# Row maxima turned by VectorE instead of TensorE, and an output projection in half-height tiles, in an attention block with a gated MLP

## The chip, the core and the metric

The kernel runs on one core of a Trainium2 chip. A core has TensorE (PE: matmuls, whose weights are loaded by a separate instruction, PEld), VectorE (DVE), ScalarE (ACT), GpSimd (POOL) and SyncE (SP, which issues most DMAs). Each engine works through its own list of instructions in order; semaphores join them. Matmul results go to PSUM, which has eight banks of 128 x 512 fp32 values. The metric is the device time of one execution in microseconds, as the median of several runs.

## What is computed

One transformer block over 2048 tokens of width 512, all in fp32, with 32 heads of 16 and an MLP of width 1376:

```python
xn = _layernorm(x)
qkv = (xn @ wqkv).reshape(B, S, 3, H, Dh)          # S 2048, H 32, Dh 16
scores = einsum("bhqd,bhkd->bhqk", q, k) * Dh ** -0.5
p = softmax(scores)
s = einsum("bhqk,bhkd->bhqd", p, v).reshape(B, S, D) @ wo
g = silu(gelu(xn @ w1 + b1) @ w2 + b2)
out = x + s * g
```

## The kernel before

**Splitting.** An fp32 product is made from rounded operands: a high part h and the rest l, and three matmuls h·h, h·l, l·h (`mm3`, L76). For the scores the three terms lie on top of each other in the contraction: 16 rows each of qh, ql, qh against kh, kh, kl, that is 48 rows.

**Units.** Queries are cut in 4 chunks of 512, heads in 8 groups of 4. A pair (group, chunk) is a unit u, 32 in all. For each unit the scores are computed twice. The first time (`s_one`, `s_op`; "S") they come out with queries on partitions, and DVE takes row maxima from PSUM (L185). The second time (`t_one`, L722; "T") they come out with keys on partitions, with two more contraction rows in which the negated maximum of the query stands, as high and low part against ones; so 50 rows. ACT takes the exponential (L724), and the weighted sums `pv_step` (L787; "V") follow on TensorE, whose 17th column gives the denominators.

**Turning the maxima.** The maxima of a unit lie as 128 queries x (4 heads x 4 query tiles). `s_end0` (L235) reduces and negates them (L240, DVE) and has POOL split them into high and low part, `nmh`, 128 x 32 (L243, L244). They are needed as rows of 512 queries. `s_end1` (L257) turns them by a matmul against an identity into 32 x 128 in a PSUM bank; `s_end2` (L262) copies them to SBUF (`mh`; ACT in the early stage, DVE afterwards) and stores them to DRAM (`mh_d`, L268). `load_mh` (L147) loads them later into the two rows of the T operand. In the early stage the bank comes from the ring of the S tiles (`s_tile`), afterwards from the ring of the T tiles (`t_tile`, L707: `ps_m` and three of `ps_t` in turn).

**Row halves.** Operands of at most 64 rows use half of the array's rows. Such matmuls are issued for rows 0 to 63 and for rows 64 to 127 (a = 0 and a = 1 in the code). When one half adds to a bank that the other has written, the second must wait until the first is done; a tiny instruction on another engine that waits for the one and releases the other is put between (`mark`, L583, on ACT or DVE; in the middle stage a POOL `nop`, L217).

**Stages.** (1) Layer norm, its transposes and the first products. (2) An order made by a planner (L290 to L323): MLP and projections in row halves (L573), into which `fill` (L546) puts S matmuls at row counts that follow from `ROWS`; a turning takes a place in this order, and `put` shifts the counts by it. The first 576 S matmuls (LEAD = 144, four each), so the maxima of the first 9 units, are made here; eight of the units are turned here. (3) A loop over 512 steps n (L944). A step has four T of unit n // 16, a V of the step before, and, until step 491, three S in whole or in halves (`ORDER`, L40). Turnings come behind a V, through `flush` (L161). `at(n, f, ..., pos)` puts other work into step n, behind the T number pos (L897).

**The output projection.** In steps 492 to 511 (DONE = 492) ten of the 16 token tiles (NW = 10) are projected, each in two steps: `w_token` (L859) rounds the tile's attention output into `oh` and `ol` (ACT, POOL), `w_mul` (L870) has six full matmuls of 128 rows per step behind the fourth T (12 per tile, L79), and `w_out` (L891) multiplies by the gate (DVE, L883), adds x (POOL, L888) and stores (SP, L889). `gate` (L845) makes silu's factor from `gx`, which `load_gx` (L834) fills; `gx` is a ring of four buffers here. Results go to the ring of the S banks, three by then. Two more tiles and the last chunk of four follow after the loop, where the last unit's division ends last.

Of the kernel before, what the change touches and what calls it, by code (L numbers as in the profile page):

```python
# [8 lines left out]
F32 = mybir.dt.float32  # L9
F32R = mybir.dt.float32r  # L10
AF = mybir.ActivationFunctionType
# [21 lines left out]
LEAD = 144  # L33
NW = 10
EARLY = 4
DONE = 492
FILL0 = 38
# [4 lines left out]
KB = 3  # L42
# [5 lines left out]
def fused(ctx: ExitStack, tc: tile.TileContext, x, wqk, wv, wo, w1, b1, w2, b2, out):  # L48
    nc = tc.nc
# [15 lines left out]
    mh_d = dpool.tile([NG * NCH, 2, GH, CH], F32, name="mh_d")  # L65

    ident_r = keep.tile([P, P], F32R, name="ident_r")
# [13 lines left out]
            if then:  # L81
                then()

    QS, QT, MX, NM, MH = {}, {}, {}, {}, {}
# [68 lines left out]
    made = [0, 0]  # L153
    done = {u: 0 for u in range(NU)}
    later, ended, errands, sent = [], [], [], set()

    def tick():
        for e in later:
            e[0] -= 1

    def flush():  # L161
        while later and later[0][0] <= 0:
            u = later.pop(0)[1]
            run_off()
            s_end1(u)
            s_end2(u)

    def at_of(job):
        u, st, p = job
# [29 lines left out]
    def s_one(a):  # L199
        made[a] += 1  # L200
        s_whole(heads[made[a] - 1], a)
# [29 lines left out]
    def run_off():  # L231
        while put_off:
            put_off.pop(0)()
# [21 lines left out]
    prog = {}  # L255

    def s_end1(u):  # L257
        pm = s_tile()[0] if "seen" in prog else t_tile()
        nc.tensor.matmul(pm[:2 * GH * NCH, :P], NM.pop(u).rearrange("p i a -> p (i a)"), ident_r, start=True, stop=True)  # L259
        MH[u] = pm  # L260

    def s_end2(u):  # L262
        mh = qring.tile([2 * GH * NCH, P], F32, name="mh", bufs=1)
        if "seen" in prog:
            nc.scalar.activation(mh, MH.pop(u)[:2 * GH * NCH, :P], AF.Copy)
        else:
            nc.vector.tensor_copy(mh, MH.pop(u)[:2 * GH * NCH, :P])
        nc.sync.dma_start(mh_d[u].rearrange("i j (q s) -> (i j q) s", s=P), mh)  # L268
        sent.add(u)

    sa = ExitStack()
# [31 lines left out]
    for j in range(len(pairs)):  # L303
        for h in range(2):
# [4 lines left out]
            due = next((i for i in range(j, len(pairs)) if is_m[i]), len(pairs))  # L309
# [212 lines left out]
    qring = ctx.enter_context(tc.tile_pool(name="qring", bufs=2, side="right"))  # L522
# [16 lines left out]

    prog.update(n=0, pe=0, seen=0)  # L540
    writer = {}
    s_when, put, row = [], [0], [0, 0]
    ndown = sum(1 for e in plan if e[0] == "down")
    ROWS = 12 * (4 * VQ + 2 * len(pairs)) + 6 * ndown - 10 + 2 * LEAD - 2 * (LEAD // 16 - 1) - FILL0

    def fill(a):  # L546
        due = FILL0 + put[0] + sum(made) * ROWS // (4 * LEAD)
        if sum(made) < 4 * LEAD and row[a] >= due and (made[0] <= made[1]) == (a == 0):
            taken()
            if later and later[0][0] <= 0:  # L550
                put[0] += 2
                u = later.pop(0)[1]
                s_end1(u)
                s_end2(u)
# [205 lines left out]
    wb = ctx.enter_context(tc.tile_pool(name="work_b", bufs=2))  # L760
# [4 lines left out]
    wo_h = kp.tile([P, KT, D], F32R, name="wo_h")  # L765
    wo_l = kp.tile([P, KT, D], F32R, name="wo_l")

    WR = {}

    def load_wo(k):  # L770
        WR[k] = wb.tile([P, 2, D], F32, name="gx", bufs=4)[:, 0]
        nc.sync.dma_start(WR[k], wo[k * P:(k + 1) * P, :])

    def wo_high(k):
# [51 lines left out]
    GX, OTS, PW, homes = {}, {}, {}, {}  # L826

    def home(i):
        if i not in homes:
            homes[i] = (slot(i, (P, KT, D)) if i < KB else  # L830
                        keep_r.tile([P, 2 * KT, D], F32, name="kt0"))
        return homes[i]

    def load_gx(t):  # L834
        i = 2 * (t % NCH)
        if t < NW:
            GX[t] = wb.tile([P, 2, D], F32, name="gx", bufs=4)
        elif t < NT - NCH:
            GX[t] = home(KB)[:, i:i + 2]
# [8 lines left out]
        nc.vector.scalar_tensor_tensor(g, e, 1.0, g, op0=OP.add, op1=OP.mult)  # L848

    def w_round(blocks, src, lo):  # L850
        oh = wb.tile([P, KT, P], F32R, name="oh", bufs=3)
        ol = wb.tile([P, KT, P], F32R, name="ol", bufs=3)
# [17 lines left out]
    def w_mul(t, ks, parts=(0, 1)):  # L870
        if t not in PW:
            PW[t] = [ps_t.tile([P, CH], F32, name="pst") if NW <= t < NT - NCH or i else
                     ps_m.tile([P, CH], F32, name="ps") if t == NT - 1 else s_tile()[0]
                     for i, cs in enumerate(cols(t))]
        for i, cs in enumerate(cols(t)):
            if i in parts:
                for k in ks:
                    mm3(PW[t][i][:, :cs.stop - cs.start], OTS[t, k], (wo_h[:, k, cs], wo_l[:, k, cs]),
                        k == 0, k == KT - 1)

    def w_gate(t, i=0):
        gx, cs = GX[t], cols(t)[i]
# [14 lines left out]
    def at(n, f, *a, pos=3):  # L897
        todo.setdefault((n, pos), []).append((f, a))

    KS = tuple(range(KT))  # L900
# [21 lines left out]
            at(16 * u + (31 if u < NU - 2 else 22), o_div, u, nc.gpsimd)  # L922
    T3 = range(NT - NCH, NT)
    late = range(NW, NT)
    for t in range(NW):
        n = DONE + 2 * t
        at(n - 4, load_gx, t)
        at(n - 2, w_token, t)
        at(n, w_mul, t, KS[:2])
        at(n, gate, t)  # L930
        at(n + 1, w_mul, t, KS[2:])
        at(n + 1, w_out, t, nc.gpsimd)
    for i, t in enumerate(late):
        n = L - 2 * len(late) - 1 + 2 * i
        at(n - 4, load_gx, t)
# [8 lines left out]
    for n in range(L + 1):  # L944
        ua, ka = divmod(n, 16)
        want = due(n) - due(n - 1)
        i = 0
# [71 lines left out]
```

## Time and profile before

| | us |
|---|---|
| median of 3 runs | 1590.88 (1590.16 to 1591.05) |
| the profiled execution: its time | 1589.65 |
| its span, first to last instruction | 1587.9 |
| matmuls of line 259 (turning), count | 32, 0.25 each |
| copies of the turned maxima | 8 on ACT (L265), 24 on DVE (L267), 0.27 each |
| DVE reductions of line 185 | 2048, 0.685 each |

The page counts an engine as busy while an instruction of it is under way, and matmuls overlap in time, so PE is shown full nearly everywhere, and the granted TensorE clock is 0.999 of full speed. In the views below, an instruction row gives start and duration, engine, line and operation, the tiles written and read, shapes (`64*128 64x512` is 64 rows by 128 columns of weights and 512 moving columns) and a count; neighbouring rows of one kind are merged, and then the duration reaches from the first start to the last end. A group's row gives busy time, mean ns of one and, behind the bar, idle time of the engine ahead of it with what released it.

### The profile page before, as it was taken

How to read it: one execution, taken by the hardware profiler on the slowest of the kernel's cores; microseconds unless marked ns; L12 is line 12 of the kernel's file. 1: busy time of each engine (PE TensorE's matmuls, PEld its weight loads, DVE VectorE, ACT ScalarE, POOL GpSimd, SP SyncE). 2: the span in 40 equal slices, each digit the busy share in tenths (PEclk: the TensorE clock that was granted, in tenths of full speed). 3: DMA queues.
4: the chain of work that ended last, by engine and by line, in shares of the span. 5: the costliest groups of instructions: out<-in, count | busy, mean ns of one | idle time of the engine just before them, and what ended most of it. 6: DMA issues, size and time to landing. Idle time of an engine off the chain costs nothing.

```text
span 1587.9 us, 32482 instructions
## 1 busy us (share of the span) xinstructions
PE 1577.7 (99%) x12146; PEld 954.9 (60%) x12146; DVE 1382.6 (87%) x2267; ACT 1256.4 (79%) x2524; POOL 378.7 (24%) x398
## 2 busy tenths in 40 slices
PE   9999999999999999999999999999999999999998
PEld 7899989999995444444444444444444444444445
DVE  7489888888988999999999999999999999999734
ACT  4333433444339999999999999999999999999984
POOL 4145575755641001001100200100010000000144
PEclk9999999999999999999999999999999999999999
DMA  6625443354422113111511411221141111110262
GB/s 206 150 59 138 131 137 98 127 154 127 130 83 75 39 33 70 31 36 35 86 31 31 69 35 37 53 49 29 27 78 26 31 29 37 35 29 22 65 198 89
DMA packets 76798, 116.93 MB, mean 74 GB/s; under 512 B 25156, under 2 KB 26436, under 8 KB 75464
## 3 DMA queue, kind: packets, MB, share of 16 engines
q1 hardware_dynamic: 73180, 102.42, 23.4%
q0 software_dynamic: 3264, 12.35, 4.1%
q8 instruction: 96, 1.57, 0.4%
q14 instruction: 62, 0.51, 0.1%
q10 hardware_dynamic: 196, 0.07, 0.0%
HBM read 84.35 MB, written 25.97 MB: 69 GB/s over the span
## 4 chain that ended last, share of the span: by engine, by line
PE 98%; DVE 1%; DMA 0%; issue 0%; ACT 0%; SPq 0%; DVEq 0%; POOLq 0%; ACTq 0%
PE pv L787 32%; PE pst L722 22%; PE ps L573 13%; PE ps L179 9%; PE pst L573 7%; PE ps L722 7%; PE ps L79 4%; PE pv L573 2%; PE pst L79 1%; DVE slot L74 0%; DMA xt<-in_x 0%; DVE st L407 0%; PE pst L259 0%; PE ps L259 0%; DVE xn L421 0%
## 5 line engine op out<-in xcount | busy, mean ns | idle before, releaser
L185 DVE TENSOR_REDUCE mx<-ps 128x2 f32<-128x512 f32 x2048 | 1299.3, 685 | 137.3 <-PE ps L179 53.3
L724 ACT ACTIVATE slot<-pst 128x512 f32<-128x512 f32 x1533 | 833.3, 612 | 5.6 <-PE ps L179 1.1
L787 PE MATMUL pv<-slot,vsb 128*17 128x512 f32 (+1 forms) x4096 | 539.2, 598 | 0.0
L179 PE MATMUL ps<-kt,slot 48*128 48x512 f32 x1364 | 383.6, 370 | 0.1
L722 PE MATMUL pst<-qt,kt 50*128 50x512 f32 x1149 | 380.1, 431 | 0.5 <-DVE gt L655 0.3
L722 PEld LDWEIGHTS pst<-qt,kt 50*128 50x128 f32 x1149 | 191.5, 184 | 264.7 <-ACT slot L724 250.6
L724 ACT ACTIVATE slot<-ps 128x512 f32<-128x512 f32 x515 | 314.8, 612 | 10.3 <-PE pst L722 7.4
L179 PEld LDWEIGHTS ps<-kt,slot 48*128 48x128 f32 x1364 | 225.1, 184 | 2.1 <-POOLq L217 0.4
L573 PE MATMUL ps<-slot,w1h 64*128 64x512 f32 x1088 | 220.4, 393 | 0.0
L179 PE MATMUL ps<-kt,qz 48*128 48x512 f32 x512 | 214.7, 420 | 0.0
L179 PE MATMUL ps<-slot,slot 48*128 48x512 f32 x598 | 167.8, 368 | 0.0
L722 PE MATMUL ps<-qt,kt 50*128 50x512 f32 x387 | 164.1, 426 | 0.0
L573 PEld LDWEIGHTS ps<-slot,w1h 64*128 64x128 f32 x1088 | 153.0, 185 | 6.8 <-ACT junk L587 1.0
L573 PE MATMUL ps<-slot,w1l 64*128 64x512 f32 x544 | 143.0, 393 | 0.0
L367 POOL TENSOR_TENSOR hl<-hg,hh 128x512 fp32r<-128x512 f32 x76 | 96.9, 1298 | 131.5 <-ACT hh L366 92.6
L722 PE MATMUL pst<-qt,slot 50*128 50x512 f32 x384 | 120.1, 426 | 0.0
L787 PEld LDWEIGHTS pv<-slot,vsb 128*17 128x17 f32 (+1 forms) x4096 | 68.7, 96 | 82.8 <-issue 29.4
L587 ACT ACTIVATE junk<-ident_r 1x1 f32<-1x1 f32 x92 | 18.0, 196 | 126.1 <-PE pst L573 122.9
L722 PEld LDWEIGHTS ps<-qt,kt 50*128 50x128 f32 x387 | 71.1, 184 | 75.5 <-ACT slot L724 57.7
L722 PEld LDWEIGHTS pst<-qt,slot 50*128 50x128 f32 x384 | 65.9, 184 | 78.0 <-ACT slot L724 73.0
L179 PEld LDWEIGHTS ps<-kt,qz 48*128 48x128 f32 x512 | 93.7, 183 | 17.9 <-DVE mx L185 0.6
L179 PEld LDWEIGHTS ps<-slot,slot 48*128 48x128 f32 x598 | 98.7, 184 | 1.0
(150 smaller groups left out, 1659.4 us busy)
## 6 DMA issues: line engine op xcount, KB each, us to landing
raw<-in_w SPq DMA_DIRECT2D x88, 256.0 KB
qk_h<-hh SPq DMA_DIRECT2D x32, 256.0 KB
qk_l<-hl SPq DMA_DIRECT2D x32, 256.0 KB
qt<-qk_h SPq DMA_DIRECT2D x128, 64.0 KB
slot<-qk_h SPq DMA_DIRECT2D x92, 64.0 KB
xt<-in_x SPq DMA_DIRECT2D x16, 256.0 KB
g_d<-gt POOLq DMA_DIRECT2D x16, 256.0 KB, 3.0
qt<-qk_l SPq DMA_DIRECT2D x64, 64.0 KB
```

The costliest lines, as they stand in the source:

```text
L79: nc.tensor.matmul(ps, lhs[a], rhs[b], start=first and n == 0, stop=last and n == 2)
L179: return nc.tensor.matmul(ps[:, c0:c0 + w], QS[u][r, p, qi * P:(qi + 1) * P], kts[u // NCH % KB][p][r, k0:k0 + w], start=True, stop=True).ins
L185: nc.vector.tensor_reduce(MX[u][:, 2 * p:2 * p + 2, qi, ki][:, heads, parts], ps.rearrange("p (n c) -> p n c", c=HC), axis=AX.X, op=OP.max)
L367: nc.gpsimd.tensor_sub(hl, raw, hh.bitcast(F32))
L573: i = nc.tensor.matmul(ps, lhs[r], rhs[r], start=first, stop=last).ins
L587: i = nc.scalar.activation(junk[:, :1], ident_r[:1, :1].bitcast(F32), AF.Copy).ins
L722: nc.tensor.matmul(ps, kts[g % KB][p][r, k * P:(k + 1) * P], QT[u][r, p, :], start=True, stop=True)
L724: nc.scalar.activation(PT[u, k][:, 2 * p + a, :], ps, AF.Exp, scale=SCALE)
L787: nc.tensor.matmul(PV[u][32 * j:32 * j + w, :], vsb[:, k, h:h + w], PT[u, k][:, j, :], start=(k == 0), stop=(k == NT - 1))
```

## The change

Maxima are turned by one DVE instruction that transposes each 32 x 32 block of the 128 x 32 tile. Block b then holds, on partition 32 b + r, row r of the maxima for the 32 queries 32 b to 32 b + 31; the store puts the blocks together in DRAM, in 128 pieces of 128 B. The matmul, the PSUM bank and the copy go; `fill` no longer gives the turning a place.

The ten token tiles are projected two at a time over four steps, in 64-row tiles: tile t on rows 0 to 63 and tile t + 1 on rows 64 to 127 for two steps, then the other way round. Each of the 12 full matmuls of a tile becomes two of 64 rows, 240 in place of 120. They stand in groups of four behind the first, second and third T of a step. A POOL `nop` waits for the last matmul of the second step, and the first ones of the third step wait for it. Loads, rounding and output of the two tiles are moved with them: `w_token` of the second tile behind the first T of the step before, both `w_out` at the end of the fourth step. `oh` and `ol` get four buffers instead of three, the `gx` ring three instead of four, and every fourth tile's `gx` lies in a buffer of the keys that is free by then.

```diff
     def fill(a):
-        due = FILL0 + put[0] + sum(made) * ROWS // (4 * LEAD)
+        due = FILL0 + sum(made) * ROWS // (4 * LEAD)
...
             if later and later[0][0] <= 0:
-                put[0] += 2
-                u = later.pop(0)[1]
-                s_end1(u)
-                s_end2(u)
-                return
+                s_end1(later.pop(0)[1])
             s_one(a)
...
     def s_end1(u):
-        pm = s_tile()[0] if "seen" in prog else t_tile()
-        nc.tensor.matmul(pm[:2 * GH * NCH, :P], NM.pop(u).rearrange("p i a -> p (i a)"), ident_r, start=True, stop=True)
-        MH[u] = pm
-
-    def s_end2(u):
-        mh = qring.tile([2 * GH * NCH, P], F32, name="mh", bufs=1)
-        if "seen" in prog:
-            nc.scalar.activation(mh, MH.pop(u)[:2 * GH * NCH, :P], AF.Copy)
-        else:
-            nc.vector.tensor_copy(mh, MH.pop(u)[:2 * GH * NCH, :P])
-        nc.sync.dma_start(mh_d[u].rearrange("i j (q s) -> (i j q) s", s=P), mh)
+        mh = qring.tile([P, 2 * GH * NCH], F32, name="mh", bufs=1)
+        nc.vector.transpose(mh, NM.pop(u).rearrange("p i a -> p (i a)").bitcast(F32))
+        nc.sync.dma_start(mh_d[u].rearrange("i j (q b s) -> b (i j q) s", b=NCH, s=2 * GH * NCH), mh)
         sent.add(u)
...
+    def w_half(t, part, third):
+        two = (t, t + 1)
+        if part == 0 and third == 0:
+            for b in two:
+                PW[b] = [s_tile()[0]]
+        side, ks = divmod(part, 2)
+        ops = [(k, i, j) for k in KS[2 * ks:2 * ks + 2] for i, j in ((0, 0), (0, 1), (1, 0))]
+        for n in (2 * third, 2 * third + 1):
+            for a in range(2):
+                b, r, (k, i, j) = two[a ^ side], slice(64 * a, 64 * a + 64), ops[n]
+                op = nc.tensor.matmul(PW[b][0], OTS[b, k][i][r], (wo_h, wo_l)[j][r, k], start=part == 0 and n == 0,
+                                      stop=part == 3 and n == 5).ins
+                if part == 2 and n == 0:
+                    tc.add_manual_dep(op, turned[t].name, SYNC, reason="other row tile")
+        if part == 1 and third == 2:
+            turned[t] = nc.gpsimd.nop().ins
+            tc.add_manual_dep(turned[t], op.name, SYNC, reason="row tile done")
...
-    for t in range(NW):
+    for t in range(0, NW, 2):
         n = DONE + 2 * t
-        at(n - 4, load_gx, t)
-        at(n - 2, w_token, t)
-        at(n, w_mul, t, KS[:2])
-        at(n, gate, t)
-        at(n + 1, w_mul, t, KS[2:])
-        at(n + 1, w_out, t, nc.gpsimd)
+        for b in range(2):
+            at(n - 3 + b, load_gx, t + b)
+            at(n - 2 + b, w_token, t + b, pos=3 * (1 - b))
+            at(n + b, gate, t + b)
+        for part in range(4):
+            for third in range(3):
+                at(n + part, w_half, t, part, third, pos=third)
+        for b in range(2):
+            at(n + 3, w_out, t + b, nc.gpsimd)
```

More of the change, by code (lines that the diff above doesn't have):

```diff
@@ L82, in mm3 @@
                 then()
-    QS, QT, MX, NM, MH = {}, {}, {}, {}, {}
+    QS, QT, MX, NM = {}, {}, {}, {}
     SYNC = mybir.DependencyInfo(mybir.DependencyClass.Sync, mybir.DependencyReason.DATA)
@@ L541, in fused @@
     writer = {}
-    s_when, put, row = [], [0], [0, 0]
+    s_when, row = [], [0, 0]
     ndown = sum(1 for e in plan if e[0] == "down")
-    ROWS = 12 * (4 * VQ + 2 * len(pairs)) + 6 * ndown - 10 + 2 * LEAD - 2 * (LEAD // 16 - 1) - FILL0
+    ROWS = 12 * (4 * VQ + 2 * len(pairs)) + 6 * ndown - 10 + 2 * LEAD - FILL0
     def fill(a):
-        due = FILL0 + put[0] + sum(made) * ROWS // (4 * LEAD)
+        due = FILL0 + sum(made) * ROWS // (4 * LEAD)
         if sum(made) < 4 * LEAD and row[a] >= due and (made[0] <= made[1]) == (a == 0):
@@ L550, in fill @@
             if later and later[0][0] <= 0:
-                put[0] += 2
-                u = later.pop(0)[1]
-                s_end1(u)
-                s_end2(u)
-                return
+                s_end1(later.pop(0)[1])
             s_one(a)
@@ L770, in load_wo @@
     def load_wo(k):
-        WR[k] = wb.tile([P, 2, D], F32, name="gx", bufs=4)[:, 0]
+        WR[k] = wb.tile([P, 2, D], F32, name="gx", bufs=3)[:, 0]
         nc.sync.dma_start(WR[k], wo[k * P:(k + 1) * P, :])
@@ L835, in load_gx @@
         i = 2 * (t % NCH)
-        if t < NW:
-            GX[t] = wb.tile([P, 2, D], F32, name="gx", bufs=4)
+        if t < NW and i < 6:
+            GX[t] = wb.tile([P, 2, D], F32, name="gx", bufs=3)
         elif t < NT - NCH:
-            GX[t] = home(KB)[:, i:i + 2]
+            GX[t] = home(KB)[:, i - 6 * (t < NW):][:, :2]
         else:
@@ L850, in w_round @@
     def w_round(blocks, src, lo):
-        oh = wb.tile([P, KT, P], F32R, name="oh", bufs=3)
-        ol = wb.tile([P, KT, P], F32R, name="ol", bufs=3)
+        oh = wb.tile([P, KT, P], F32R, name="oh", bufs=4)
+        ol = wb.tile([P, KT, P], F32R, name="ol", bufs=4)
         n = len(blocks)
@@ L879, in w_mul @@
                         k == 0, k == KT - 1)
+    turned = {}
+    def w_half(t, part, third):
[15 more added lines that the diff above has]
+            tc.add_manual_dep(turned[t], op.name, SYNC, reason="row tile done")
     def w_gate(t, i=0):
```

## The prediction

> **What bounds the kernel now.** I read the page first (its span and its chain of waits), then four stretches of the span side by side, then the order of time on TensorE (PE) at one place of each stretch.
>
> ```profile
> span 1587.9 us, 32482 instructions
> PE 98%; DVE 1%; DMA 0%; issue 0%; ACT 0%; SPq 0%; DVEq 0%; POOLq 0%; ACTq 0%
> 50.00:470.00 420.00, 420.00 (x3482) 380.04 (x3482) 364.42 (x572) 158.13 (x357) 235.97 (x207) 1.00 0.42 121
> 500.00:1480.00 980.00, 980.00 (x7602) 464.29 (x7602) 907.38 (x1495) 974.40 (x1926) 75.11 (x123) 1.00 0.19 40
> 1500.00:1563.00 63.00, 63.00 (x349) 29.20 (x347) 23.35 (x27) 53.82 (x106) 28.14 (x21) 1.00 0.47 155
> ```
>
> The last three rows are windows: start and end, length, then busy time and count of PE, of its weight loads, of DVE, ACT and POOL, then the granted clock. The chain that ends last is 98% PE, so what counts is how densely PE starts its matmuls. Early (50 to 470) PE alone is full; in the middle (500 to 1480) ACT is called busy for 974 of 980 us and DVE for 907; late (1500 to 1563) PE is full, ACT and DVE are not. A busy share doesn't say whether PE could go faster, so I take the distance between starts.
>
> **Part 1, the turning of the maxima: 32 matmuls go.** In the early stage two streams run side by side, one on array rows 0 to 63, one on rows 64 to 127:
>
> ```profile
> 115.13 0.39 PE L573 MATMUL pv<-w2h,hl 64*128 64x512 f32 x1
> 115.23 0.39 PE L573 MATMUL pst<-w2h,hl 64*128 64x512 f32 x1
> 115.55 0.25 PE L259 MATMUL ps<-ident_r,nmh 128*32 128x128 f32 x1
> 115.73 0.50 PE L573 MATMUL pst<-w2h,hh 64*128 64x512 f32 x2
> 116.07 0.39 PE L573 MATMUL pst<-w2l,hh 64*128 64x512 f32 x2
> ...
> 116.77 0.39 PE L573 MATMUL pv<-w2h,hh 64*128 64x512 f32 x1
> 116.77 0.39 PE L573 MATMUL pst<-w2l,hh 64*128 64x512 f32 x1
> 117.00 0.39 PE L179 MATMUL ps<-kt,qz 48*128 48x512 f32 x1
> ```
>
> Undisturbed, two matmuls start every 0.23 us (116.77, 117.00); I call that a slot. Around the turning matmul (L259, which uses all 128 rows) the pairs start at 115.13 and 115.23, then 115.73, then 116.07. Without it the second pair after the first would start at 115.59 and 115.69: the delay is 0.48 on one half and 0.38 on the other, mean 0.43. Eight units are turned in this stage: 8 x 0.43 = 3.4 us.
>
> In the middle stage the matmul stands between the weighted sums (L787) of one step and the scores of the next:
>
> ```profile
> 528.95 1.05 PE L787 MATMUL pv<-slot,vsb 128*17 128x512 f32 x8
> 529.93 0.25 PE L259 MATMUL pst<-ident_r,nmh 128*32 128x128 f32 x1
> 531.24 1.05 PE L787 MATMUL pv<-slot,vsb 128*17 128x512 f32 x8
> 533.25 1.05 PE L787 MATMUL pv<-slot,vsb 128*17 128x512 f32 x8
> 1391.91 1.01 PE pv L787 x8
> 1408.18 1.00 PE pv L787 x8
> ```
>
> The last two rows are from the chain and eight steps of one unit apart, so an ordinary step is 2.03 us. The one with the turning takes 2.29, and the one after it 2.01, 0.02 short. The excess over the two is 0.24; I take 0.22, rounded down for the spread of such steps, and it comes 23 times: 5.1 us. Part of it is the accumulator bank that the turning takes out of the scores' rotation. The last unit's turning falls in the late stage, where the projection groups start as follows:
>
> ```profile
> 1499.71 1.59 PE ps L79 x6
> 1503.33 1.59 PE ps L79 x6
> 1506.57 1.57 PE ps L79 x6
> ...
> 1561.55 1.60 PE ps L79 x6
> ```
>
> 3.62 against 3.24, so 0.4 us more.
>
> **What takes its place.** A DVE transpose of 128 x 32. The trace has none, so I bound it: between nothing and one large reduction, a third of 1.89 = 0.63 us; I take 0.28, like the small reduction L240, the row nearest in size.
>
> ```profile
> L240 DVE TENSOR_REDUCE nm<-mx 128x16 f32<-128x128 f32 x32 | 8.8, 276 | 0.1
> L815 DVE RECIPROCAL dr<-dr 128x16 f32<-128x16 f32 x32 | 7.8, 243 | 2.2 <-DMA dr<-os 2.2
> 530.68 1.89 DVE L185 TENSOR_REDUCE mx<-ps 128x2 f32<-128x512 f32 x3
> 528.98 0.22 POOL L244 TENSOR_TENSOR nmh<-nm,nmh 128x16 fp32r<-128x16 f32 x1
> ```
>
> In the last 24 units it replaces a DVE copy; in the first eight ACT did that copy and DVE gets new work, at most 8 x 0.63 = 5 us in a stage where it is free for 56. Cover in the middle: three reductions take 1.89 of 2.03 us, so the 16 steps of a unit leave 2.2, less 0.28 and 0.24 for L240 and L815: 1.7 us, more than the dearest transpose. Its price is nothing; were the cover gone, 23 x 0.28 = 6 us. Behind a late transpose wait DVE's next reductions, and behind these the banks of the other scores. Its input is there in time: POOL finished the low parts at 529.20, before L259 ran.
>
> The store of a turned unit becomes 128 pieces of 128 B instead of 32 of 512 B. The nearest row is the store of the reciprocals, 128 pieces of 64 B, and what SP could issue after it:
>
> ```profile
> 1504.21 1.36 SPq L150 DMA_DIRECT2D qt<-mh_d  x2
> 1568.37 0.33 SPq L816 DMA_DIRECT2D den_d<-dr  x1
> 1570.11 1.72 SPq L819 DMA_DIRECT2D dn<-den_d  x4
> ```
>
> 1.74 us from its issue to the dependent load. The tightest unit is the last: its load (1504.21) is issued by 1505.57 and first used in the step whose projection starts two groups after 1506.57, about 1513. Some tenths more, up to the whole 1.74 again, vanish in that.
>
> **Part 2, the projection of ten tiles.** A late step before:
>
> ```profile
> 1504.85 1.05 PE L787 MATMUL pv<-slot,vsb 128*17 128x512 f32 x8
> 1505.83 0.49 PE L722 MATMUL ps<-qt,kt 50*128 50x512 f32 x1
> 1505.84 0.73 PE L722 MATMUL pst<-qt,kt 50*128 50x512 f32 x3
> 1506.50 0.50 PE L79 MATMUL ps<-wo_h,oh 128*128 128x512 f32 x1
> 1507.75 0.39 PE L79 MATMUL ps<-wo_h,ol 128*128 128x512 f32 x1
> 1508.07 1.05 PE L787 MATMUL pv<-slot,vsb 128*17 128x512 f32 x8
> ```
>
> From the sums to the scores 0.98; four scores, two to a row half, as two slots 0.67; six full matmuls 1.57. That is 3.22, and the mean of seventeen steps (1506.57 to 1561.55) is 3.23. Eight slots would be 1.84; the other 0.40 of 0.67 + 1.57 lies where the shape changes: 0.1 on entry from the sums (a first slot is 0.34, as from 115.73 to 116.07), 0.2 on the way from 64 rows to 128, and 0.09 on the way to the sums (1507.75 to 1508.07 is 0.32).
>
> After it, the twelve half matmuls of a step and its four scores are eight per row half, again eight slots, and no shape changes between them. The step becomes 0.98 + 0.34 + 6 x 0.23 + 0.32 = 3.02, which is 0.21 less: 20 x 0.21 = 4.2 us. The unknown price is that of a half matmul: 0.115 us if two run side by side (as at 116.77), 0.23 if they don't. I take the first, from rows of the same kind: 64 rows, 512 columns, separate banks.
>
> The order within one half must not hold up the other. The program issues two scores on rows 64 to 127, then two on rows 0 to 63; yet the second to start does so 0.01 us after the first (1505.84), and the last of the four ends 0.73 after that, so with 0.39 of its own it starts 0.34 after. Four in two slots: one of the later two was pulled ahead. A rule speaks against this: the Trainium skill ("TensorE: Matmul & The Clock Gate", section "The mechanism") says that weight loads are pulled ahead but matmuls start strictly in program order. By the rule part 2 would bring about nothing (rival a); these rows contradict it.
>
> **New waits of part 2.** Halfway the two tiles swap halves, and a POOL nop passes the word from the last matmul of the second step to the first of the third. The middle stage uses the same device in every step:
>
> ```profile
> L179 PEld LDWEIGHTS ps<-kt,slot 48*128 48x128 f32 x1364 | 225.1, 184 | 2.1 <-POOLq L217 0.4
> L883 DVE SCALAR_TENSOR_TENSOR gx<-ps,gx 128x512 f32<-128x512 f32 x10 | 6.9, 692 | 17.5 <-PE ps L79 17.5
> L888 POOL TENSOR_TENSOR gx<-gx 128x512 f32<-128x512 f32 x10 | 13.4, 1343 | 12.9 <-DVE gx L883 12.8
> ```
>
> PE lost 0.4 us to it in the whole run. Here a score and the sums (1.3 us) stand between. On POOL the nop is queued behind the two final additions of the pair before: these end 0.69 + 2 x 1.34 = 3.4 us after that pair's last matmul, and the nop is due two steps (6 us) after it, so 2.6 us are spare. Behind the nop wait the next pair's low parts, wanted a step later. A pair's second bank is the one that the earlier pair's first gating frees: 0.69 us, against 0.32 + 0.98 from that pair's last slot to the next scores. I count both at nothing; some tenths, five times, is the other bound. ACT does the same operations in another order: 53.8 of 63 us are 2.8 of 3.23 a step, under 3.02. SP gets the two output stores of a pair together, behind the additions; what follows there is a load that is wanted three steps on. In the tail POOL has one addition more ahead of its last subtraction, about a us, before an operand that PE wants only after another tile's twelve matmuls (12 x 0.23 = 2.8 us).
>
> **Sum.** 3.4 + 5.1 + 0.4 + 4.2 = 13.1 us. Made against the profiled execution, 1589.65 us (span 1587.9 and 1.75 around it): 1576.6. That execution lies 1.2 below the median of the runs, 1590.88, so the forecast for the median is 1577.8.
>
> **Rivals.** (a) Matmuls keep program order across the halves. With 1 for rows 64 to 127, a new step issues 1 0101 1 0101 0 0101 0; where two neighbours share a half, the other half idles, which makes nine slots, 0.23 more, and eats the 0.21. Then only part 1 counts: 1590.9 - 8.9 = 1582. Against it stands 1505.84. (The Trainium skill's rule above, "The mechanism" in "TensorE: Matmul & The Clock Gate", would have it so.) (b) The middle is bound by ACT (974 of 980), and the 5.1 aren't gained: 1583. Against it:
>
> ```profile
> 1506.85 1.57 ACT L724 ACTIVATE slot<-pst 128x512 f32<-128x512 f32 x3
> ```
>
> Three exponentials, each about 0.6 long, in 1.57: one every 0.49, four in 1.95, less than 2.03. (c) The swap waits: POOL is late by one addition, 1.34 us, in each of five pairs: 1577.8 + 6.7 = 1584.5. For it: POOL has everything in one queue; against it: the 2.6 us. (d) Slower: half matmuls don't run side by side, because both streams read halves of the same weights. Then a step has six slots more and saves only the shape changes: 1.38 - 0.2 = 1.18, times 20 is 23.6, less the 8.9 of part 1: 1606. It decides from a half matmul of 0.17 us on (12 x 0.17 - 1.38 - 0.2 = 0.46 a step, which eats the 8.9). Against it: L573, where two streams also read halves of one tile, two every 0.23.
>
> **Chances.** Forecast 0.70 (1573.5 to 1581), (a) 0.07, (b) 0.08, (c) 0.06, (d) and whatever else ends slower 0.09. The range 1573.5 to 1585 takes in (a) to (c). No change can be told within 0.2%, 3.2 us. Faster 0.88, same 0.03, slower 0.09.
>
> **What would show it.** No L259; middle steps with a transpose at 2.03; early pairs 0.23 apart throughout; late sums 3.02 apart; half matmuls two every 0.23; next to no wait of PE for POOL's queue in the late stage. It would be wrong if DVE stands idle ahead of a transpose, if late steps stay above 3.2, or if middle steps grow elsewhere.

## The result, and the profile after

| us | before | after |
|---|---|---|
| median of four runs each | 1590.79 (1590.16 to 1591.05) | 1576.91 (1576.49 to 1577.64) |
| span of the profiled execution | 1587.9 | 1574.7 |

The ratio is 0.9914 (0.9897 to 0.9931), so the kernel became 13.9 us, 0.9%, faster. The forecast was 1577.8.

The page of the kernel after, its chain of waits by engine, and the windows of the middle and the late stage that answer to those of before (start and end, length, busy time and count of PE, PEld, DVE, ACT and POOL, granted clock, DMA):

```profile
span 1574.7 us, 32597 instructions
PE 98%; DVE 1%; DMA 0%; issue 0%; ACT 0%; SPq 0%; POOL 0%; DVEq 0%; ACTq 0%
495.00:1475.00 980.00, 980.00 (x7617) 466.21 (x7616) 909.38 (x1502) 977.93 (x1935) 74.93 (x123) 1.00 0.19 40
1489.00:1550.00 61.00, 61.00 (x485) 31.46 (x488) 20.23 (x29) 56.17 (x108) 27.32 (x22) 1.00 0.51 170
```

These views alone say little: PE is full in each stage as before, the clock is the same, and the chain is PE's. What changed is how far apart PE's starts lie. So I cut the span at the same pieces of work in both kernels. The first two rows of each fence are two groups of row-half matmuls; "52.7 to 98.8" is the start of the first and of the last of a group. The early stage is counted from the first start of the one group to the last start of the other (52.7 to 481.1). The other rows are weighted sums (V) on PE's timeline. Before:

```profile
L573 PE MATMUL pst<-kt,slot x192: 383/391/502, 52.7 to 98.8; 64*128 64x512 f32 x192
L573 PE MATMUL pst<-w2h,hl x264: 383/390/494, 102.9 to 481.1; 64*128 64x512 f32 x132
485.69 1.05 PE L787 MATMUL pv<-slot,vsb 128*17 128x512 f32 x8
...
1495.13 1.05 PE L787 MATMUL pv<-slot,vsb 128*17 128x512 f32 x8
1497.62 1.05 PE L787 MATMUL pv<-slot,vsb 128*17 128x512 f32 x8
1501.22 1.05 PE L787 MATMUL pv<-slot,vsb 128*17 128x512 f32 x8
...
1563.07 1.91 PE L787 MATMUL pv<-slot,vsb 128*17 128x512 f32 x16
```

After:

```profile
L560 PE MATMUL pst<-kt,slot x192: 384/391/498, 53.4 to 99.0; 64*128 64x512 f32 x192
L560 PE MATMUL pst<-w2h,hl x264: 383/391/418, 103.3 to 476.2; 64*128 64x512 f32 x132
480.75 1.05 PE L774 MATMUL pv<-slot,vsb 128*17 128x512 f32 x8
...
1485.47 1.05 PE L774 MATMUL pv<-slot,vsb 128*17 128x512 f32 x8
1488.96 1.05 PE L774 MATMUL pv<-slot,vsb 128*17 128x512 f32 x8
1492.00 1.05 PE L774 MATMUL pv<-slot,vsb 128*17 128x512 f32 x8
...
1549.89 1.91 PE L774 MATMUL pv<-slot,vsb 128*17 128x512 f32 x16
```

| stretch | before | after | difference | forecast |
|---|---|---|---|---|
| ahead of the first row-half matmul | 52.7 | 53.4 | +0.6 | 0 |
| early stage | 428.4 | 422.8 | -5.6 | -3.4 |
| the steps with S, from the second V to that of step 490 | 1009.44 | 1004.72 | -4.7 | -5.1 |
| step 491, the last with S | 2.49 | 3.49 | +1.0 | 0 |
| 20 late steps (first 3.60 to 3.04, nineteen 61.85 to 57.89) | 65.45 | 60.93 | -4.5 | -4.6 |
| from the last such V to the end | 24.8 | 24.8 | 0 | 0 |

They add up to 13.2, the difference of the spans; the piece between the early stage and the second V, 4.5 and 4.6, is not in the table. The start ahead of the first row-half matmul is no part of the change: over the kernels below it lies anywhere from 52.5 to 53.6, and at 55.3 in the one with six transposes.

The new instructions by tile (shortest, median and longest in ns, then first and last start) and a late step on PE's timeline, both of the kernel after:

```profile
L258 DVE STREAM_TRANSPOSE mh<-nmh x32: 200/202/205, 117.0 to 1493.9; 128x32 f32<-128x32 f32 x32
L259 SPq DMA_DIRECT2D mh_d<-mh x32: 522/572/673, 117.2 to 1494.2; - x32
```

```profile
1510.29 1.05 PE L774 MATMUL pv<-slot,vsb 128*17 128x512 f32 x8
1511.27 0.50 PE L709 MATMUL ps<-qt,kt 50*128 50x512 f32 x1
...
1511.61 0.38 PE L880 MATMUL ps<-wo_l,oh 64*128 64x512 f32 x1
...
1512.07 0.40 PE L709 MATMUL pst<-qt,kt 50*128 50x512 f32 x1
1512.07 0.39 PE L880 MATMUL ps<-wo_h,oh 64*128 64x512 f32 x1
...
1513.00 0.40 PE L709 MATMUL pst<-qt,kt 50*128 50x512 f32 x1
...
1513.33 0.62 PE L774 MATMUL pv<-slot,vsb 128*17 128x512 f32 x4
```

The transpose takes 0.20 us. In the late step two matmuls start together, one on each row half (1512.07 twice), and a pair of them every 0.23: 0.98 from the sums to the scores, 0.34 for the first slot, six slots in 1.39 (1511.61 to 1513.00) and 0.33 to the next sums make 3.04.

Step 491 is the one stretch that became longer. Timeline of PE, ACT and POOL there, kernel after; the bracket is idle time ahead of the instruction and its releaser:

```profile
1486.88 0.65 ACT L841 ACTIVATE oh<-slot 128x512 fp32r<-128x512 f32 x1
1487.61 2.51 POOL L842 TENSOR_TENSOR ol<-slot,oh 128x512 fp32r<-128x512 f32 x2 [23.51 <-PE pst L709]
1487.88 0.66 ACT L841 ACTIVATE oh<-slot 128x512 fp32r<-128x512 f32 x1
1488.65 0.38 PE L178 MATMUL ps<-kt,slot 48*128 48x256 f32 x1 [1.07 <-POOLq L216]
```

The step's last S half-matmul stood still for 1.07 us. It waits for the POOL `nop` of its step (L216), which is issued behind the first S (`ORDER`). Ahead of that in POOL's queue stand both subtractions of the first pair, one placed behind the last T of step 490 and one behind the first T of step 491, and each waits for its rounding on ACT. The second rounding ends at 1487.88 + 0.66 = 1488.54, and the matmul starts 0.11 later, at 1488.65, while the subtractions are still under way. So what is late is ACT's second rounding, and POOL's queue hands the wait on to PE. Before, only the first token's subtraction stood ahead of that `nop`: step 491 was 2.49 there, 0.46 over an ordinary step, and is 1.46 over it now.

### The profile page after: what moved, and what is told of

Read it like the earlier page. It is cut to its first block, busy times and chain, and to the rows that moved or that the text cites. A ratio compares the mean times of both kernels' runs of the same rounds, so it can differ in the third digit from the quotient of the medians.

```text
span 1574.7 us, 32597 instructions
## 1 busy us (share of the span) xinstructions
PE 1563.7 (99%) x12234; PEld 954.6 (61%) x12234; DVE 1377.5 (87%) x2275; ACT 1254.2 (80%) x2516; POOL 378.0 (24%) x398
## 4 chain that ended last, share of the span: by engine, by line
PE 98%; DVE 1%; DMA 0%; issue 0%; ACT 0%; SPq 0%; POOL 0%; DVEq 0%; ACTq 0%
PE pv L774 32%; PE pst L709 16%; PE ps L709 14%; PE ps L560 13%; PE ps L178 9%; PE pst L560 7%; PE pv L560 2%; PE ps L79 2%; PE ps L880 1%; PE pst L79 1%; DVE slot L74 0%; DMA xt<-in_x 0%; DVE st L398 0%; DVE xn L412 0%; DVE slot L890 0%
## 5 line engine op out<-in xcount | busy, mean ns | idle before, releaser
L711 ACT ACTIVATE slot<-pst 128x512 f32<-128x512 f32 x1533 | 809.6, 616 | 2.1 <-PE ps L709 0.8
L709 PE MATMUL pst<-qt,kt 50*128 50x512 f32 x1149 | 311.1, 406 | 0.5 <-DVE gt L642 0.3
L709 PEld LDWEIGHTS pst<-qt,kt 50*128 50x128 f32 x1149 | 211.6, 184 | 30.1 <-ACT slot L711 11.0
L709 PE MATMUL ps<-qt,kt 50*128 50x512 f32 x387 | 190.7, 495 | 0.0
L709 PE MATMUL pst<-qt,slot 50*128 50x512 f32 x384 | 102.3, 406 | 0.0
L242 POOL CAST nmh<-nm 128x16 fp32r<-128x16 f32 x32 | 6.3, 197 | 353.5 <-PE pst L709 176.4
```

What stands on the lines that cost most here:

```text
L242: nc.gpsimd.tensor_copy(hl[:, 0], nm)
L709: nc.tensor.matmul(ps, kts[g % KB][p][r, k * P:(k + 1) * P], QT[u][r, p, :], start=True, stop=True)
L711: nc.scalar.activation(PT[u, k][:, 2 * p + a, :], ps, AF.Exp, scale=SCALE)
```

## The experiments

The kernel before, run beside them on the same chips, took 1590.0 to 1590.5. Where only one run is named there is no interval, and I read the trace's steps rather than the total.

**Each part by itself.** Part 1 alone has the new `s_end1` and `fill`, part 2 alone has `w_half`, the new placing and the buffers.

```diff
 part 1 alone
+        nc.vector.transpose(mh, NM.pop(u).rearrange("p i a -> p (i a)").bitcast(F32))
...
 part 2 alone
+                at(n + part, w_half, t, part, third, pos=third)
```

> Part 1 alone: maxima turned by DVE, the projection as before. By the forecast 3.4 + 5.1 + 0.4 us less than before, 1590.8 - 8.9 = 1581.9, and by the trace of the changed kernel (first weighted sums 4.9 us earlier, middle stage 4.7 us shorter) about 1580.9. First weighted sums near 478, ordinary middle steps 2.03, late steps 3.23 as before. Rival, the parts help each other (the late stage gains because the rotation of the scores' banks is no longer shifted): then late steps of under 3.2 and a time below 1579. Rival, the gain is all of part 2: above 1586.

> Part 2 alone: the turning by matmul stays. Late steps 3.05 instead of 3.23 make 19 x 0.19 = 3.6 us less, and the step in which the first pair is rounded (491) costs some 0.4 us net: 1590.8 - 3.2 = 1587.6. First weighted sums at 483, as before. If the parts add up, the two gains of these runs make 13.2 to 13.9 together. Rival, part 2 gains only with part 1: 1590 or more.

Part 1 alone: 1579.99 (1579.24 to 1580.26), ratio 0.9934 (0.9920 to 0.9947). Its early stage is 423.0 and its middle 1004.65, as with both parts; its step 491 is 2.47 and its late steps stay at 3.235. Part 2 alone: 1587.38 (1586.49 to 1587.90), ratio 0.9979 (0.9970 to 0.9988). Its early stage stays at 428.7, its late steps are 3.05 (the second, with the last turning, 3.22), and step 491 is 3.48. So the parts act in separate stretches: 10.5 and 3.1 add up to 13.6, against 13.9 measured together. The lost microsecond of step 491 belongs to part 2.

**The turning matmul put back beside the transpose.** It writes a bank that nobody reads.

```diff
     def s_end1(u):
+        pm = s_tile()[0] if "seen" in prog else t_tile()
+        nc.tensor.matmul(pm[:2 * GH * NCH, :P], NM[u].rearrange("p i a -> p (i a)"), ident_r, start=True, stop=True)
```

> The changed kernel with the turning matmul issued as well, into a bank that nobody reads; the transpose still supplies the maxima. What comes back is the price of the matmul on TensorE and of its bank alone. By the forecast 8 x 0.43 early and 23 x 0.22 in the middle: 1576.9 + 8.9 = 1585.8, with the first weighted sums 3.4 us later than in the changed kernel (481.5). Rival: part of the early gain (4.9 us, forecast 3.4) comes from the turning's place in the order of the two streams and from ACT's copy, which don't come back here; then the first weighted sums come under 481.5 and the time is under 1585.8, but above 1584. If the bank was nothing, a middle step with the matmul takes 2.21; with it 2.27.

It took 1586.99, so 10.1 of the 10.5 us of part 1 came back, more than the forecast's 8.9, and the first weighted sums came at 483.4 instead of 481.5. My rival, that less than 8.9 would come back, is refuted as well. A middle step of this kernel with the matmul in it (PE's timeline):

```profile
529.34 1.05 PE L776 MATMUL pv<-slot,vsb 128*17 128x512 f32 x8
530.32 0.25 PE L258 MATMUL pst<-ident_r,nmh 128*32 128x128 f32 x1
531.62 1.05 PE L776 MATMUL pv<-slot,vsb 128*17 128x512 f32 x8
```

2.28, against 2.03 of an ordinary step. Over the 23 middle steps with a turning the mean is 2.25 here, 2.25 before and 2.03 in the kernel after: the matmul and its bank together are the whole of the middle stage's excess, and the copy that followed is no part of it. What the bank alone costs stays open, since 2.25 lies between the 2.21 and 2.27 that were to tell it. In the early stage, where this kernel's order gives the matmul no place of its own, it costs 5.7 us for eight (428.5 against 422.8), all that the early stage had gained.

**Its place in the early order kept, without the matmul.** The row counts of before return, and a turning takes a turn of `fill` again.

```diff
-        due = FILL0 + sum(made) * ROWS // (4 * LEAD)
+        due = FILL0 + put[0] + sum(made) * ROWS // (4 * LEAD)
...
+                put[0] += 2
                 s_end1(later.pop(0)[1])
+                return
+            taken()
```

> The changed kernel with the turning's place in the early order kept, but empty: the transpose goes to DVE, the S matmul still comes one place later and the row counts shift as before. Early stage (first to last matmul of its row-half line): 428.4 us before, 422.8 after; at the eight turnings 0.25 to 0.5 each are lost at once, and as much again between them. If the place (the shifted order) costs that other part: about 425.5, first weighted sums near 480.8. If the matmul costs it all: 422.8 and 478.1.

The early stage took 424.6 (its first row-half matmul starts at 53.1, its last at 477.7), the whole 1577.96. That lies between the two values that I had set. With the place left in the order, taking the matmul out gains 3.8 us (8 x 0.47); taking out the empty place as well gains 1.8 more (8 x 0.23, one slot each). This split holds for this order of the two only. The kernel with the matmul put back has no place, and its early stage is as long as before: there the place's absence gains nothing, and the matmul costs 0.71 each. Only the two together give the 5.6.

**The kernel before with its eight early copies on DVE.** This tells whether freeing ACT of them is what the early stage gained by.

```diff
-        if "seen" in prog:
-            nc.scalar.activation(mh, MH.pop(u)[:2 * GH * NCH, :P], AF.Copy)
-        else:
-            nc.vector.tensor_copy(mh, MH.pop(u)[:2 * GH * NCH, :P])
+        nc.vector.tensor_copy(mh, MH.pop(u)[:2 * GH * NCH, :P])
```

> The kernel before, but the eight early copies of the turned maxima are DVE's instead of ACT's. If ACT, which waits in order for the turning matmul ahead of that copy, holds back what frees the two streams' banks, the early stage gets some 2.5 us shorter (426, first weighted sums at 480.6, 1588). If not: 428.4, 483.1 and 1590.

1590.48, the early stage 428.3: no difference. ACT's copies play no part.

**Each transpose six times.** The last one leaves the result that is stored.

```diff
-        nc.vector.transpose(mh, NM.pop(u).rearrange("p i a -> p (i a)").bitcast(F32))
+        for _ in range(6):
+            nc.vector.transpose(mh, NM[u].rearrange("p i a -> p (i a)").bitcast(F32))
```

> The changed kernel with each transpose made six times over (0.2 us each, so 1.0 us more on DVE per unit). By the forecast's cover (1.7 us of free DVE time per unit of the middle stage, 1.5 after one transpose) this costs nothing: 1577, middle steps 2.03. Rival, the cover counts only as far as the scores' banks reach at the one place where the transposes stand: then that step grows by 0.5 to 0.9, 23 times, 1588 to 1598; early, where DVE has room, nothing.

It took 1611.30, beyond both the forecast and the rival. First DVE's timeline around one transpose of the kernel after, then DVE's and PE's of this kernel around six:

```profile
523.38 1.89 DVE L184 TENSOR_REDUCE mx<-ps 128x2 f32<-128x512 f32 x3
525.18 0.20 DVE L258 STREAM_TRANSPOSE mh<-nmh 128x32 f32<-128x32 f32 x1
525.39 1.89 DVE L184 TENSOR_REDUCE mx<-ps 128x2 f32<-128x512 f32 x3
```

```profile
537.65 1.44 DVE L259 STREAM_TRANSPOSE mh<-nmh 128x32 f32<-128x32 f32 x6
539.01 1.85 DVE L184 TENSOR_REDUCE mx<-ps 128x2 f32<-128x512 f32 x3
```

```profile
538.36 1.05 PE L775 MATMUL pv<-slot,vsb 128*17 128x512 f32 x8
541.45 1.05 PE L775 MATMUL pv<-slot,vsb 128*17 128x512 f32 x8
```

Three reductions hold DVE for 1.80 us (523.38 to 525.18), so a step of 2.03 leaves it 0.23, and one transpose, 0.21 (525.18 to 525.39), just fits. Six hold it for 1.36 (537.65 to 539.01), 1.15 more, and the step takes 3.09 instead of 2.03: nearly the whole lateness is passed on, by the S banks, whose reductions start late. In that step three weight loads of S wait for DVE's reductions, 0.19, 0.41 and 0.30 us. The step after it takes 2.02 (its sums start at 543.47), so nothing is won back. Over the middle stage the loss is 23.1 us for 23 units, 1.00 each. The early stage loses too, against the rival: 432.6 against 422.8, which is 1.23 for each of eight. The chain of waits of this kernel shows DVE at 9%, where the kernel after has 1%.

**All half matmuls of the projection on rows 0 to 63.**

```diff
-                b, r, (k, i, j) = two[a ^ side], slice(64 * a, 64 * a + 64), ops[n]
+                b, r, (k, i, j) = two[a ^ side], slice(0, 64), ops[n]
```

> The changed kernel with all half matmuls of both tiles on rows 0 to 63 (the upper half of the contraction is left out, the lower one used twice), so that none can run beside another. Rows 0 to 63 then hold 12 half matmuls and two scores of a step, 14 slots in place of 8: late steps 3.05 + 6 x 0.23 = 4.43, the whole 20 x 1.38 = 27.6 us longer, about 1604.5. Rival, the two streams gain nothing by running side by side (a half matmul costs 0.115 alone as well): 3.05 and 1577.

1604.38. A late step of this kernel (PE's timeline; "x2" are two in a row, the durations reach over both):

```profile
1511.24 1.05 PE L774 MATMUL pv<-slot,vsb 128*17 128x512 f32 x8
...
1512.80 0.63 PE L880 MATMUL ps<-wo_l,oh 64*128 64x512 f32 x2
1513.27 0.62 PE L880 MATMUL ps<-wo_h,ol 64*128 64x512 f32 x2
...
1515.68 1.06 PE L774 MATMUL pv<-slot,vsb 128*32 128x512 f32 x8
```

Two half matmuls on one half take 0.47, so 0.23 each, and the step is 4.44. In the kernel after the same two share one slot of 0.23.

**The half matmuls in blocks of six.** Six on rows 0 to 63 behind the first score (which is on rows 64 to 127), then the second score, again on rows 64 to 127, then the six of that half.

```diff
-        for n in (2 * third, 2 * third + 1):
-            for a in range(2):
+        for a in (third,) if third < 2 else ():
+            for n in range(6):
...
-        if part == 1 and third == 2:
+        if part == 1 and third == 1:
```

> The changed kernel with another order: behind the first score of a step all six half matmuls of rows 0 to 63, behind the second all six of rows 64 to 127, none behind the third. Each half still has eight slots. If a half's matmuls start as soon as that half is free, however far down the list: 3.05 per late step and 1577. If matmuls start strictly in program order, the halves run one after the other, 13 slots: 3.05 + 5 x 0.23 = 4.2, 1577 + 23 = 1600. In between, the chip looks a limited number of instructions ahead, and the step says how many.

1583.36, late steps of 3.38, so neither theory was right in full. PE's timeline of this kernel:

```profile
1513.39 0.49 PE L709 MATMUL ps<-qt,kt 50*128 50x512 f32 x1
1513.39 0.49 PE L880 MATMUL ps<-wo_h,oh 64*128 64x512 f32 x1
...
1513.95 0.40 PE L880 MATMUL ps<-wo_h,ol 64*128 64x512 f32 x1
1513.96 0.50 PE L709 MATMUL pst<-qt,kt 50*128 50x512 f32 x1
1514.19 0.51 PE L880 MATMUL ps<-wo_h,oh 64*128 64x512 f32 x2
```

In program order the second score (1513.96) comes behind six half matmuls of the other half. It started together with the third of them, ahead of the fourth to sixth (from 1514.19 on). So PE does start a matmul ahead of earlier ones when it is on the other half, but not at once: with no limit it would have started in the slot after the first score, at 1513.72. What limits it is not shown. Nor did its reader gain by the early start: in every late step the exponential of this score starts 1.73 to 1.74 us after the first score, about when the sixth of those half matmuls is done (in the step before this one at 1511.75 on ACT's timeline, with 0.50 idle ahead of it, released by L880), though the score itself started at 0.57 to 0.59.

**Full matmuls of 128 rows in the places of the half ones**, one tile after the other.

```diff
-            for a in range(2):
-                b, r, (k, i, j) = two[a ^ side], slice(64 * a, 64 * a + 64), ops[n]
...
+            b, (k, i, j) = two[side], ops[n]
+            nc.tensor.matmul(PW[b][0], OTS[b, k][i], (wo_h, wo_l)[j][:, k], start=part % 2 == 0 and n == 0,
+                             stop=part % 2 == 1 and n == 5)
```

> The changed kernel with 6 full matmuls per step (128 rows, one tile after the other) in the places of the 12 half ones: two behind each of the first three scores. Scores stand alone then, so 4 + 6 = 10 slots where there were 8, and six more changes between 64 and 128 rows where the kernel before had one on that way. By the theory a change costs 0.2 for a pair of them there and back or more each way: 0.98 + 10 x 0.23 + 0.3 + 6 x 0.1 to 0.2 = 4.2 to 4.8 per late step, so 1600 to 1612. Rival, a change of shape costs nothing and the 0.2 us of the step before were something else: 0.98 + 2.3 + 0.3 = 3.6, 1588.

1608.84, late steps of 4.67. PE's timeline of this kernel between two scores:

```profile
1512.92 0.50 PE L709 MATMUL ps<-qt,kt 50*128 50x512 f32 x1
1513.34 0.51 PE L880 MATMUL ps<-wo_h,oh 128*128 128x512 f32 x1
1513.69 0.40 PE L880 MATMUL ps<-wo_l,oh 128*128 128x512 f32 x1
1514.01 0.50 PE L709 MATMUL pst<-qt,kt 50*128 50x512 f32 x1
```

0.42, 0.35 and 0.32 where three undisturbed slots are 0.69: a change from 64 rows to 128 and back costs 0.40. So with full matmuls in the same places the kernel is 18 us slower than before, although part 1 is in it; what part 2 gains, it gains by the halves.

**No swap.** Each tile stays on its half of the rows, without the `nop`.

```diff
-                b, r, (k, i, j) = two[a ^ side], slice(64 * a, 64 * a + 64), ops[n]
+                b, r, (k, i, j) = two[a], slice(64 * a, 64 * a + 64), ops[n]
...
-        if part == 1 and third == 2:
-            turned[t] = nc.gpsimd.nop().ins
-            tc.add_manual_dep(turned[t], op.name, SYNC, reason="row tile done")
```

> The changed kernel without the swap: each tile stays on its row half for all four steps (half of the contraction is left out, the other half used twice), so no nop and no wait on it. By the theory the swap costs nothing: late steps 3.04 to 3.05 as with it, 1577. Rival, the word through POOL is late: the steps with a swap, every fourth, were the 3.06 ones, and up to 5 x 0.02 to 0.1 us is gained.

1576.86, and nineteen late steps in 57.9, as in the kernel after. The swap costs nothing.

**The first pair's rounding moved forward.** High parts on ACT in steps 486 and 488, behind the step's fourth T; low parts on POOL in 488 and 490, behind the second T.

```diff
+            if t:
+                at(n - 2 + b, w_token, t + b, pos=3 * (1 - b))
+            else:
+                at(n - 6 + 2 * b, w_high, b)
+                at(n - 4 + 2 * b, w_low, b, pos=1)
```

> The changed kernel, with the first two tiles' rounding moved: high parts in steps 486 and 488, low parts (POOL) in 488 and 490 behind the nop of that step. Theory: in step 491 the nop that joins the halves of a score stood behind a 1.3 us subtraction, which made that step 3.49 instead of 2.03; behind the nop the subtraction fits into the 2.03 us to the next one, so steps 488 to 491 take 2.0 to 2.1 and the whole is up to 1.4 us shorter, less what the first late step gave back (0.5): 1575.5 to 1576.4. Rival, ACT's extra rounding makes the step long, not POOL: then the excess moves to steps 486 to 489 and the time stays at 1576.9.

1576.13 (1575.68 to 1578.05), ratio 0.9915 (0.9902 to 0.9929). PE no longer waits for POOL and step 491 is 2.02, but two steps behind a rounding are longer instead, 2.48 and 2.40. The first of them, timeline of ACT and PE of this kernel:

```profile
1478.66 0.65 ACT L852 ACTIVATE oh<-slot 128x512 fp32r<-128x512 f32 x1
1479.28 1.05 PE L774 MATMUL pv<-slot,vsb 128*17 128x512 f32 x8
1480.84 0.18 PEld L709 LDWEIGHTS pst<-qt,kt 50*128 50x128 f32 x1 [0.28 <-ACT slot L711]
1481.76 1.05 PE L774 MATMUL pv<-slot,vsb 128*17 128x512 f32 x8
```

The rounding puts the exponentials back, and this score waits for its bank (0.28), the next one again (0.30): ACT's rounding had its own share in step 491, as the rival said, beside the wait through POOL. Within the spread of its runs this kernel can't be told from the kernel after.

**The same, with the high parts on POOL too**, four POOL instructions in steps 485 to 488, each behind the step's `nop`.

```diff
-        nc.scalar.activation(oh, ot[c][:, :, i * P:(i + 1) * P], AF.Copy)
+        nc.gpsimd.tensor_copy(oh, ot[c][:, :, i * P:(i + 1) * P])
...
-                at(n - 6 + 2 * b, w_high, b)
-                at(n - 4 + 2 * b, w_low, b, pos=1)
+                at(n - 7 + 2 * b, w_high, b, pos=1)
+                at(n - 6 + 2 * b, w_low, b, pos=1)
```

> As the run with the first pair's rounding moved, but the high parts are rounded by POOL too, so ACT gets nothing more: four POOL operations of 1.3 us in steps 485 to 488, each behind the nop of its step. In the former run two steps of 2.48 and 2.40 were left (0.9 us over 2.03), without a wait for POOL: if ACT's rounding made them, these go and the whole is 0.9 us shorter, about 1575.2. Rival, POOL's operation itself makes them (a nop or a port): then four steps are over 2.3 and the time is not below 1576.

1574.94 (1574.46 to 1575.39), ratio 0.9905 (0.9888 to 0.9921), the fastest of all, with no run as slow as the fastest of the kernel after. Its V:

```profile
1484.91 1.05 PE L774 MATMUL pv<-slot,vsb 128*17 128x512 f32 x8
1486.95 1.05 PE L774 MATMUL pv<-slot,vsb 128*17 128x512 f32 x8
```

All steps up to 491 (the last here, 1484.91 to 1486.95) are at 2.02 to 2.04. The last is 1.46 less than 3.49, all that step 491 had over an ordinary one. The other half microsecond of the difference in span lies ahead of the first row-half matmul, which starts at 52.8 here.

## Why the prediction was right, and which steps of it were not

The direction, the four stretches in which the time is gained, and the total held. Several terms inside were off, and that the total met the runs within 1 us is in part luck: 2.2 us too little in the early stage stand against 0.4 too much in the middle, 1.0 lost in step 491 and 0.6 in the start.

- **Early turning, 8 x 0.43 = 3.4: too small, measured 5.6.** The step counted what the rows around one matmul show. With the place kept, taking the matmul out gives 3.8, so that reading held within 0.4. The rest, 1.8, comes only when the place of its own in the order of `fill` goes too, as it does in the change. The diff shows it (`put`, `return`), the prediction's local rows can't, and it was costed at nothing without being named. The two don't add: with the matmul there, the place costs nothing (428.5 without it, 428.4 with it). Why an empty place costs just a slot (0.23), and a matmul without a place three (0.71), stays open.
- **Middle, 23 x 0.22 = 5.1: measured 4.7.** The kernel with the matmul put back, whose middle stage is 5.1 longer than that of the kernel after, shows that it is the matmul and its bank. The 0.4 missing is 0.02 a step.
- **The transpose at nothing: right in the outcome, wrong in its reason.** It said "Cover in the middle" leaves "1.7 us, more than the dearest transpose". Six transposes in place of one, 1.15 more and under 1.7, cost 1.00 a unit. DVE's free time in sixteen steps can't be saved up and spent in one: what counts is the room in that place, 0.23 a step, and about a tenth beyond it. The transpose was free because at 0.21 it fits into that room, as the reciprocal of 0.24 does (L802, in whose steps the mean is 2.03). The 0.28 that I took for it came from L240, which reads four times as many elements (128 x 128 against 128 x 32), and was too much. No run lies between one transpose and six; if what is over 0.23 were passed on whole, 0.28 would have cost up to 23 x 0.05 = 1.2 us and the upper bound, 0.63, up to 23 x 0.40 = 9.2, most of what part 1 gains (an estimate from these rows). The second case, 1587, lay outside the range of 1573.5 to 1585.
- **The store** takes SP 0.57 us to issue instead of 0.31 to 0.38. Nobody waited for it, as forecast.
- **Late steps, 20 x 0.21 and 0.4 for the last turning: 4.6 forecast, 4.5 measured, and here two misses cancel.** The step's build-up of 0.98, 0.34, six slots and 0.32 was met term by term within 0.01, but an ordinary late step went from 3.235 to 3.047, which is 0.19 and not 0.21: 3.8 in all. The last turning was worth 0.38, as forecast (3.62 before, 3.24 in part 1 alone). The other 0.36 is the first late step, 3.60 before and in part 1 alone, which the forecast took for an ordinary one. Before, its fourth score waits 0.31 for ACT (at 1499.21), which is behind since the first tile's rounding in step 491; after, it is 3.04. The term at stake, 0.115 for a half matmul, is settled by the kernel with all of them on one half: 4.44 a step.
- **Edits counted at nothing that were not: the first pair's rounding.** The prediction asked what stands on POOL ahead of the swap's `nop`, and there it was right: no wait in the late stage. It did not ask what the moved `w_token` of the second token stands ahead of. In step 491 that is the middle stage's own `nop`, the device that it quoted as harmless; the 0.4 us of that row, the only such wait before, was the same place with one rounding ahead of it. Price 1.0 us in step 491, of which the first late step gave back 0.36. The last experiment takes the whole back, and the 0.46 of before with it.

**The rivals.** (a) Program order across the halves, 1582: refuted, by the late steps and by a score that started ahead of three earlier matmuls. The rule of the Trainium skill ("TensorE: Matmul & The Clock Gate", section "The mechanism"), that matmuls start in program order, does not hold here across row halves; but the pull is limited, and the order in the program still costs 0.33 a step when six of a half are put in a row. (b) ACT bounds the middle, 1583: refuted by 4.7. Yet it was near: four exponentials in 1.95 of 2.03 leave 0.08 a step, and one rounding of 0.65 on ACT cost 0.45 in the kernel with the first pair moved. (c) The swap waits, 1584.5: refuted by the kernel without the swap, which has the same late steps. (d) No halves side by side, 1606: this was built as a kernel, 1604.4, and the change is not it. The shape changes that part 2 avoids are there, 0.40 there and back. By the Trainium skill ("TensorEngine Tiling (Array Packing)", section "Key Properties") a change of the tiling mode drains TensorE; the time that these rows lose agrees with that.

## What to carry to other kernels

Free time of an engine counts in the place where the new work stands, not as a sum over a loop: if the engine that sets the pace can't catch up afterwards, lateness there is passed on nearly whole (1.00 of 1.15 us here). When a diff takes away an instruction, look also for the place that the order kept for it, and don't expect the two to add; when it moves work on a side queue, list every token or `nop` that shares this queue in the step where it lands, and what the moved work itself waits for. In this kernel operands of 64 rows paid for their double count where they stood among other work of that height and alternated between the halves closely; in blocks of six they lost 0.33 a step, and all on one half 1.39.

## What the runs showed of the hardware that was not expected

- A matmul on one row half is started ahead of earlier matmuls on the other half, but only a few: behind six of them it passed three (1513.96 against 1514.19), 0.24 later than the slot after the score before it (1513.72). What reads it starts only about when the six are done (1.73 after the first score, in all twenty late steps).
- A change between 64-row and 128-row matmuls takes 0.40 us there and back (0.42, 0.35 and 0.32 in place of 0.23 each).
- The block transpose of 128 x 32 fp32 on DVE takes 200 to 205 ns, less than the small reduction from 128 x 128 to 128 x 16 (276 ns on the page of before).
- A store in 128 pieces of 128 B keeps SP 0.57 us at its issue (median of 32, after), one of 32 pieces of 512 B 0.31 us (before).
